# A fused attention and mixture-of-experts kernel: operands of x kept in SBUF over four experts, with tokens grouped by chunk position

## The chip, the cores and the metric

The kernel runs on one core of a Trainium2 chip. The metric is the device time of one execution in microseconds (us). Three runs of the kernel before took 1182.35, 1184.10 and 1184.86 us; the median, 1184.1 us, is the time that the change is measured against.

## The reference

The first half is a decayed linear attention, the second a weighted sum of four two-layer networks over its result. All data are 32-bit floats.

```python
# q, k, v: (4 sequences, 8 heads, 768 positions, 64); blocks of 64 positions, one after the other
intra = (qb @ kb.T * Dmask) @ vb            # within the block, Dmask[i, j] = lam ** (i - j) for i >= j
inter = (qb * lam_pow) @ kv_state           # from all blocks before; kv_state starts at zero
out_block = intra + inter
kv_state = lam_block * kv_state + (kb * rev_pow).T @ vb
# x = out, tokens by features: (3072, 512)
p = domain_probs / (domain_probs.sum(-1) + 1e-9)
out = sum(p[:, e:e+1] * (relu(x @ w1[e]) @ w2[e]) for e in range(4))   # w1: 512 x 1024, w2: 1024 x 512
```

## The kernel before, in words

**Tiling.** A chunk is 128 positions of one sequence, all eight heads: two blocks of the reference. There are 24 chunks, six for each sequence. Eight chunks (1024 tokens) make a group, and there are three groups. The chunks go sequence by sequence, so group 0 holds sequence 0 and the first two chunks of sequence 1. A chunk's attention has three parts, `turn` (q and k are transposed, by TensorE, or for eight late chunks by VectorE from rows that came through a DRAM tensor `across`; GpSimd scales k in `decayed`), `scores` (products of q and k, and of k and v for the state) and `values` (L627: L643 is the product of q with the carried state, L659 that of the scores with v). The result goes to the tile `xT` (L309), which holds one group.

**Two products, as Strassen schemes.** For a group g and an expert e, `first_product` (L897) makes relu(x @ w1) and `second_product` (L958) makes the product with w2 and adds it, times the gate, to the group's result (L986, L989). Each is a seven-product (Strassen-Winograd) scheme, M1 to M7, and each of first_product's seven is split in seven once more. So first_product needs for every M seven blocks of x (128 x 256 each) and seven of w1. These are differences and sums of blocks of the input. `prepare_x` (L314) and `inner_x` (L203) compute those of x on GpSimd, for group 0 `own_x` (L1231) does on VectorE, and all are stored to a DRAM tensor `x_ops` (L129). The weights' operands are prepared by GpSimd in the same way and stored to `w1_ops`. For every expert, group and M, `feed` (L824) fetches 896 KB of `x_ops` (L832) and then 896 KB of `w1_ops` (L834), each into a tile of a pool `stream` with two buffers for each kind.

The hidden result of first_product stays in SBUF in blocks A11, A12, A21, A22. `operands` (L706) makes S1 to S4 of them on VectorE as soon as a block is complete, in tiles of their own ("hS"), from a pool of 48 tiles. `second_product` takes these in the order SEQ2 (L939), M1, M2, M7, M6, M4, M5, M3. For the last group the second product is turned round and also split twice (`nested_product`, L1199).

**Order of the work.** The order on every engine is written out by the kernel; nothing is rescheduled. The units (group, expert) go one after the other. In each unit the second product of this unit is interleaved with the first product of the next: seven steps (one M of each), each of eight slots, in which four parts of the second product and seven of the first alternate (L1540). In each slot the loop also takes one piece of VectorE work from a list `background` (`rest`, L510), may run one step of the next group's attention (`attention`, L680, at places that PLACES, L678, lists by step and slot), and calls `pump` (L150). This starts the next piece of preparation ("chore") when a running estimate of GpSimd's busy time lets it, and issues stores that are due. At the first slot of a step, the operands of the next step's M are fetched (L1564). In unit 0 a list `own_sums` gives one subtraction of `own_x` a slot. Group 0's attention, at the start, is interleaved with the first parts of a plain seven-product scheme for expert 0 (`direct_product`), in a list by hand.

SP issues nearly all DMAs, in this order, and a DMA that has to wait for a buffer or for data holds those behind it. `give_across` (L1107) writes a part of the last group's result at the very end, transposed on VectorE and in eight DMAs for M3.

Of the kernel before, what the change touches and what calls it, by code (L numbers as in the profile page):

```python
# [17 lines left out]
NPOOL = 48  # L18
AHEAD = 2
# [3 lines left out]
def kernel(  # L23
# [30 lines left out]
    nc = tc.nc  # L54
# [20 lines left out]
    stage = ctx.enter_context(tc.tile_pool(name="stage", bufs=8))  # L75
    w2pool = ctx.enter_context(tc.tile_pool(name="w2", bufs=6))
    stream = ctx.enter_context(tc.tile_pool(name="stream", bufs=2))
    opool = ctx.enter_context(tc.tile_pool(name="o", bufs=CPG))
# [15 lines left out]

    def tt(eng, o, a, b, op):
        eng.tensor_tensor(out=o, in0=a, in1=b, op=op)  # L96
        if eng is nc.gpsimd:
            busy[0] = max(busy[0], now[0]) + math.prod(o.shape[1:]) / 480
# [10 lines left out]

    nat = {}  # L110

    def load(n, names="qkv"):

        b, c = divmod(n, NCH)
        for name in names:
            x = small(f"{name}n")
# [12 lines left out]
    x_ops = dram.tile([NG, 7, P, 7, 256], FP32, name="x_ops")  # L129
# [4 lines left out]
    X_AT = {n: i for i, n in enumerate(("M1", "M7", "M6", "M4", "M5", "M2", "M3"))}  # L134
# [67 lines left out]

    def inner_x(eng, g, m, blk):  # L203
        at = {"B11": (0, 0), "B12": (0, 1), "B21": (1, 0), "B22": (1, 1)}
        inner(eng, ("x", g, m), x_ops[g, MS.index(m)], blk, T_OPS, at)
# [103 lines left out]
    xT = consts.tile([P, 4, G], FP32, name="xT")  # L309

    b11, b21 = xT[:, 0:2, 0:W], xT[:, 2:4, 0:W]
    b12, b22 = xT[:, 0:2, W:G], xT[:, 2:4, W:G]

    def prepare_x(g):  # L314

        st = {}

        def total(name, a, b, op):
            t = stage.tile([P, 2, W], FP32, name="xo", tag="st")
            halves(t[:], a, b, op)  # L320
            st[name] = t[:]

        def ready(m, blk):
            inner_x(nc.gpsimd, g, m, blk)

        return [lambda: ready("M1", b11), lambda: ready("M2", b21)], [
            lambda: total("T1", b12, b11, ALU.subtract), lambda: ready("M5", st["T1"]),
            lambda: total("T2", b22, st["T1"], ALU.subtract), lambda: ready("M6", st["T2"]),
            lambda: total("T3", b22, b12, ALU.subtract), lambda: ready("M7", st["T3"]),
            lambda: ready("M3", b22),  # L330
            lambda: total("T4", b21, st["T2"], ALU.subtract), lambda: ready("M4", st["T4"]),
        ]


# [29 lines left out]
    ACROSS = {2: 2, 3: 2}  # L364
    across = dram.tile([B, 2, P, NHP, NCH * 4, 32], FP32, name="across")
    pieces = []

    def bring_across(b):
        c = ACROSS[b]
        for x, of in enumerate((q, k)):  # L370
            for y in range(4):
                for ac in range(NHP):
                    src = of[b, 4 * (y // 2) + ac, c * C:, (y % 2) * 32:(y % 2 + 1) * 32]
                    to = across[b, x, y * 32:(y + 1) * 32, ac, c * 4:]
                    pieces.append(lambda to=to, src=src: nc.sync.dma_start(
                        out=to, in_=src.rearrange("(t p) d -> p t d", p=32),
                    ))

    def trickle(m=1):
        for _ in range(m):  # L380
            if pieces:
                pieces.pop(0)()

    def comes_across(n):
        b, c = divmod(n, NCH)
        return b in ACROSS and c >= ACROSS[b]

    def load_across(n):
        b, c = divmod(n, NCH)
        for x, name in enumerate("qk"):  # L390
# [3 lines left out]
                in_=across[b, x, :, :, c * 4:c * 4 + 4].rearrange("p h t d -> p h (t d)"),  # L394
# [3 lines left out]
    def load_more(n):  # L398
        if not comes_across(n):
            load(n)  # L400
        else:
            trickle(len(pieces))
            load_across(n)
            load(n, "kv")
# [11 lines left out]
    zeros = xT[:, 3, G - P:]  # L416
# [15 lines left out]
    s_decay = consts.tile([P, 2, NHP, BL], FP32, name="s_decay")  # L432
# [11 lines left out]
    q_decay = consts.tile([P, NHP, BL], FP32, name="q_decay")  # L444
# [14 lines left out]
    def scale_q(qs, qT):  # L459
        by = q_decay[:].unsqueeze(2).to_broadcast([P, NHP, 2, BL])  # L460
# [6 lines left out]
    gate = consts.tile([P, NTOK // P, E], FP32, name="gate")  # L467


    gate_rows = dram.tile([CPG, E, P], FP32, name="gate_rows")  # L470
    gate_bc = xT[:, 0].rearrange("p (n t) -> p n t", t=C)
# [9 lines left out]

    def turn_gates():
        p, o = bank("s0", "gp"), small("gr")
        n = CPG * E
        nc.tensor.transpose(out=p[0:n, 0:P], in_=gate[:, LAST * CPG:].rearrange("p n e -> p (n e)"), identity=ident[:])
# [9 lines left out]
    background = []  # L495
    aside = []
# [17 lines left out]
    def soon(n, *work):  # L514

        background[0:0] = work
        if n < CPG:
            rest(len(work))

    def decayed(n):  # L520

        kn = nat[n, "k"]
        if comes_across(n):
            kd = kn
        else:
            kd = small("kd")[:].rearrange("p (h d) -> p h d", d=D)
# [6 lines left out]
    def begin_state(n):  # L533
        if n % NCH == 0 and n not in states:
            states[n] = small("kv")[:].rearrange("p (x h d) -> p x h d", x=2, d=D)
            nc.vector.memset(states[n][:, 0], 0.0)
        if n % NCH and n in states and n not in carried:
# [16 lines left out]
    def turn(n, tags):  # L554
# [5 lines left out]
        decayed(n)  # L560
        qn, kn = nat.pop((n, "q")), nat.pop((n, "k"))
        qp = bank(tags[0], "qp")
        kp = bank(tags[1], "kp")
        for x, y in ((qp, qn), (kp, kn)):
            for ac in range(NHP):
# [3 lines left out]
                )  # L569
        qT, kT, qs = small("qT"), small("kT"), small("qs")  # L570
# [6 lines left out]
    def scores(n, tags):  # L577
        all_added()
        while n not in turned:
            rest(force=True)  # L580
# [3 lines left out]
        first, last = n % NCH == 0, n % NCH == NCH - 1  # L584
# [33 lines left out]
        def end():  # L618
            s = states[n + 1] = small("kv")[:].rearrange("p (x h d) -> p x h d", x=2, d=D)
# [7 lines left out]
    def values(n, tags):  # L627
# [3 lines left out]
        st, work = masked.pop(n)  # L631
        while any(f in background for f in (*scaled, *work)):
            rest(force=True)
        state = states.pop(n)
        c = n % CPG
# [12 lines left out]
        for a in range(2):  # L648
            for r in range(2):
                inter(a, r, 1 - r, a == 0)  # L650
        for a in range(2):
            for r in range(2):
                inter(a, r, r, False)
        for r in range(2):
            for a in range(2):
                for x in range(2):
                    for y in range(2):
# [5 lines left out]
                        )  # L663
        for x in range(2):
            o = xT[:, :, c * C + x * BL:c * C + (x + 1) * BL]
            nc.scalar.copy(out=o, in_=op[x][:, 0:4 * BL].rearrange("p (a t) -> p a t", t=BL))
            o = o[:, 2 * (1 - x):2 * (1 - x) + 2]
            p = op[1 - x][:, 4 * BL:6 * BL].rearrange("p (a t) -> p a t", t=BL)
            adds.append((now[0], lambda o=o, p=p: tt(nc.vector, o, o, p, ALU.add)))

    FEW = tuple((i, 5) for i in range(7))
    MANY = (0, 5), (1, 2), (1, 5), (2, 5), (3, 2), (3, 5), (4, 5), (5, 2), (5, 5), (6, 5)
    WIDE = (0, 2), (0, 5), (1, 5), (2, 2), (2, 5), (3, 5), (4, 2), (4, 5), (5, 5)

    def places(**units):
        return [(int(at[1:]) * 7 + i, x) for at, of in units.items() for i, x in of]

    PLACES = {1: places(u0=FEW[2:], u1=MANY, u2=WIDE), 2: places(u3=FEW, u4=MANY, u5=MANY[:7])}  # L678

    def attention(g):  # L680

        steps = []
        early, late = prepare_x(g)
        for n in range(g * CPG, (g + 1) * CPG):
            steps.append(lambda n=n: turn(n, ("s0", "s1")))
            steps.append(lambda n=n: scores(n, ("s0", "s1")))

            def end(n=n):
                if n == g * CPG:
                    for m in MS:  # L690
                        until(("x", g - 1, m))
                values(n, ("s0", "s1"))
                if n + AHEAD < B * NCH:
                    load_more(n + AHEAD)
                if n % (CPG // 2) == CPG // 2 - 1:
# [906 lines left out]
```

## Time and profile before

| what | value |
|---|---|
| median of three runs | 1184.1 us |
| profiled execution, as a run | 1181.85 us |
| its span, first to last instruction | 1180.0 us |
| TensorE matmul busy | 98%, 8159 records |
| VectorE, ScalarE, GpSimd busy | 68%, 23%, 55% |
| DMA: moved, mean rate | 324.45 MB, 275 GB/s |
| share of the 16 DMA engines, SP's queue | 82.4% |
| mean granted TensorE clock | 0.997 |

A "record" is one instruction of the trace. A group of equal instructions has its place in the code, what it writes and reads, their shape and number; a wait names the engine and line that waited and what ended the wait, its total, how often, and the longest. In an answer in order of time, the first number is the start and the second the duration, both in us; "x8" means eight records merged, and square brackets hold the idle time of the engine ahead of them. PE is TensorE's matmul, PEld its weight load, DVE VectorE, ACT ScalarE, POOL GpSimd, SP the engine that issues DMAs, and SPq an issue. An issue's time on SP is short; the data land later (the page gives the median).

### The profile page before, as it was taken

How to read it: one execution, taken by the hardware profiler on the slowest of the kernel's cores; microseconds unless marked ns; L12 is line 12 of the kernel's file. 1: busy time of each engine (PE TensorE's matmuls, PEld its weight loads, DVE VectorE, ACT ScalarE, POOL GpSimd, SP SyncE). 2: the span in 40 equal slices, each digit the busy share in tenths (PEclk: the TensorE clock that was granted, in tenths of full speed). 3: DMA queues.
4: the chain of work that ended last, by engine and by line, in shares of the span. 5: the costliest groups of instructions: out<-in, count | busy, mean ns of one | idle time of the engine just before them, and what ended most of it. 6: DMA issues, size and time to landing. Idle time of an engine off the chain costs nothing.

```text
span 1180.0 us, 21215 instructions
## 1 busy us (share of the span) xinstructions
PE 1160.9 (98%) x8159; PEld 1009.9 (86%) x8159; DVE 798.7 (68%) x1411; ACT 275.2 (23%) x507; POOL 651.4 (55%) x624
## 2 busy tenths in 40 slices
PE   8999999999999899999999999999999999999998
PEld 7888888888878788888888888888888888888887
DVE  4796796678468647747856765764665676777785
ACT  3342122013111101311220120121243342341331
POOL 2848258347557920064445655416684683783884
PEclk9999999999999999999999999999999999999999
DMA  9798799999999997899998899898986657566543
GB/s 207 202 267 239 248 310 329 336 348 315 363 339 338 319 324 227 259 308 299 324 318 268 285 306 316 283 302 305 314 281 239 256 194 279 200 248 238 214 162 89
DMA packets 265621, 324.45 MB, mean 275 GB/s; under 512 B 121488, under 2 KB 206896, under 8 KB 265520
## 3 DMA queue, kind: packets, MB, share of 16 engines
q1 hardware_dynamic: 254912, 320.27, 82.4%
q10 hardware_dynamic: 10608, 2.82, 1.2%
q8 instruction: 65, 1.06, 0.4%
q14 instruction: 36, 0.29, 0.1%
HBM read 237.69 MB, written 89.54 MB: 277 GB/s over the span
## 4 chain that ended last, share of the span: by engine, by line
PE 86%; DMA 7%; DVE 4%; POOL 2%; issue 1%; SPq 0%; ACT 0%; ACTq 0%; DVEq 0%; POOLq 0%
PE pg L919 35%; PE q L973 28%; PE pq L1199 13%; PE pM L1334 2%; PE pc L1334 2%; DMA w2b<-in_moe_w_dram 2%; DMA ws_in<-w_ops 2%; POOL ops L96 1%; DVE m L96 1%; PE sp L591 1%; PE op L643 1%; DMA w_ops<-ops 1%; DMA w_sums<-w2o 1%; DMA w_ops<-w1o 1%; PE sp L598 1%; PE op L659 1%
## 5 line engine op out<-in xcount | busy, mean ns | idle before, releaser
L919 PE MATMUL pg<-xs_in,ws_in 128*128 128x256 f32 x1960 | 471.3, 380 | 6.7 <-DMA ws_in<-w_ops 6.4
L919 PEld LDWEIGHTS pg<-xs_in,ws_in 128*128 128x128 f32 x1960 | 371.9, 190 | 60.0 <-issue 5.0
L96 DVE TENSOR_TENSOR m<-pg,m 128x512 f32<-128x512 f32 x451 | 307.3, 687 | 98.2 <-PE pg L919 90.5
L973 PE MATMUL q<-w2t,hS 128*128 128x256 f32 x1024 | 243.5, 381 | 0.0
L973 PEld LDWEIGHTS q<-w2t,hS 128*128 128x128 f32 x1024 | 193.1, 190 | 26.5
L989 DVE SCALAR_TENSOR_TENSOR acc<-q,gate,acc 128x256 f32<-128x256 f32 x192 | 92.5, 482 | 162.4 <-PE q L973 162.0
L973 PE MATMUL q<-w2t,m 128*128 128x256 f32 x768 | 183.1, 381 | 0.0
L973 PEld LDWEIGHTS q<-w2t,m 128*128 128x128 f32 x768 | 145.0, 190 | 20.2
L931 ACT ACTIVATE m<-m 128x512 f32<-128x512 f32 x132 | 82.9, 631 | 281.0 <-DVE m L96 280.3
L96 POOL TENSOR_TENSOR m<-m,xT 128x512 f32<-128x512 f32 x64 | 80.6, 1275 | 73.6 <-ACT m L931 41.6
L96 DVE TENSOR_TENSOR sums<-pq,sums 128x256 f32<-128x256 f32 x153 | 64.2, 422 | 46.2 <-PE pq L1199 39.2
L96 POOL TENSOR_TENSOR ops<-w2b 128x256 f32<-128x256 f32 x24 | 18.8, 804 | 136.8 <-DMA w2b<-in_moe_w_dram 128.1
L927 ACT COPY m<-pg 128x512 f32<-128x512 f32 x88 | 51.6, 586 | 181.2 <-PE pg L919 170.4
L1199 PE MATMUL pq<-acc,w2t 128*128 128x256 f32 x352 | 86.6, 379 | 0.0
L1199 PEld LDWEIGHTS pq<-acc,w2t 128*128 128x128 f32 x352 | 66.8, 190 | 9.3 <-issue 0.3
L96 POOL TENSOR_TENSOR w2o<-w2b 128x512 f32<-128x512 f32 x32 | 41.0, 1303 | 44.5 <-DMA w2b<-in_moe_w_dram 25.9
L96 POOL TENSOR_TENSOR acc<-hT,hT 128x512 f32<-128x512 f32 x32 | 40.3, 1275 | 30.3 <-PE pq L1199 28.4
L862 ACT ACTIVATE m<-m 128x512 f32<-128x512 f32 x44 | 27.8, 631 | 106.5 <-DVE m L96 106.5
L96 DVE TENSOR_TENSOR hS<-m,m 128x512 f32<-128x512 f32 x56 | 44.7, 799 | 6.5 <-ACT m L931 6.5
L96 DVE TENSOR_TENSOR m<-m,m 128x512 f32<-128x512 f32 x56 | 48.2, 861 | 0.0
L96 POOL TENSOR_TENSOR acc<-hT,acc 128x512 f32<-128x512 f32 x32 | 40.7, 1273 | 7.4 <-PE pq L1199 5.4
L96 POOL TENSOR_TENSOR ops<-w1b 128x256 f32<-128x256 f32 x24 | 20.6, 878 | 43.6 <-PE pg L919 22.6
(166 smaller groups left out, 1375.7 us busy)
## 6 DMA issues: line engine op xcount, KB each, us to landing
xs_in<-x_ops SPq DMA_DIRECT2D x70, 896.0 KB, 6.4
ws_in<-w_ops SPq DMA_DIRECT2D x70, 896.0 KB, 8.4
w2t<-w_ops SPq DMA_DIRECT2D x66, 256.0 KB, 6.9
w2t<-w_sums SPq DMA_DIRECT2D x64, 256.0 KB, 4.2
w_ops<-ops SPq DMA_DIRECT2D x28, 512.0 KB, 7.3
w2t<-in_moe_w_dram SPq DMA_DIRECT2D x48, 256.0 KB, 4.4
w2b<-in_moe_w_dram SPq DMA_DIRECT2D x32, 256.0 KB, 6.0
w_sums<-w2o SPq DMA_DIRECT2D x16, 512.0 KB, 6.0
```

What stands on the lines that cost most here:

```text
L96: eng.tensor_tensor(out=o, in0=a, in1=b, op=op)
L591: nc.tensor.matmul(out=sp[r][half[x], ac * BL:(ac + 1) * BL], lhsT=hc(kT)[half[r], ac, blk[x]], rhs=hc(qT)[half[r], ac, blk[x]], start=(ac ...
L598: nc.tensor.matmul(out=sp[x][half[r], 256 + ac * D:256 + (ac + 1) * D], lhsT=kd[half[x], 2 * ac + r], rhs=vn[half[x], 4 * r + ac], start=F ...
L643: nc.tensor.matmul(out=op[r][half[y], cols(a, r) if x == r else apart(a)], lhsT=state[half[r], x, 2 * a + y], rhs=by_block(qs)[half[r], 2 ...
L862: nc.scalar.activation(out=o[:], in_=o[:], func=AF.Relu)
L919: nc.tensor.matmul(out=p[:, j * 256:(j + 1) * 256], lhsT=ws[i][:, j * P:(j + 1) * P], rhs=xs[i], start=(fresh and j == 0), stop=True, skip ...
L927: nc.scalar.copy(out=new[at][:], in_=p[:])
L931: nc.scalar.activation(out=new[at][:], in_=new[at][:], func=AF.Relu)
L973: nc.tensor.matmul(out=p[:, s * DH:(s + 1) * DH], lhsT=h[A_OF[m]][:, c * 256 + s * P:c * 256 + (s + 1) * P], rhs=fed2[g, e, m][uu][:, c], ...
L989: nc.vector.scalar_tensor_tensor(out=o, in0=x, scalar=w, in1=o, op0=ALU.mult, op1=ALU.add)
L1199: nc.tensor.matmul(out=p[:, 0:256], lhsT=fed3[e, m, x // 2][:, x % 2, c * P:(c + 1) * P], rhs=b[B_OF[i]][:, c * 256:(c + 1) * 256], start= ...
L1334: nc.tensor.matmul(out=p[:, s * 256:(s + 1) * 256], lhsT=a[c][:, f:f + P], rhs=b[:, c, j * 256:(j + 1) * 256], start=(s == 0 and c == 0 an ...
```

## The change

**Groups.** A group is now two chunk positions of all four sequences: chunks 0 and 1 of each in group 0, 2 and 3 in group 1, 4 and 5 in group 2. States of four sequences are carried side by side. Chunk position 0 has no state before it, so `values` leaves out that half of the product with the state. All chunks of group 2 come through `across`, in pieces for each sequence.

**Operands of x stay.** Seven tiles `slots`, one for each M, hold the seven blocks for first_product over all four experts. Group 0's attention writes into four of them directly, and `x_steps` makes the blocks by subtractions in place. For groups 1 and 2, `pair_sums` (GpSimd) makes the outer sums for every two chunks and stores them to `x_blocks` in DRAM; `x_fill` fetches one M's four blocks (two DMAs of 256 KB) into its slot after the last group's use of it, from step 18 and step 43 on, one M a step, and `x_inner` makes the inner differences on GpSimd. `feed` fetches weights alone.

**Room for it.** The common pool goes from 48 to 41 tiles and the stage pool from 8 to 7. The hidden operands are made in place: S3 over A21 when the block is complete, S2 over S3, S1 over A11 and S4 over A12 by `later_operands`, in the step after the last use of what they overwrite; SEQ2 is M1, M7, M4, M6, M2, M5, M3.

**Chunks at fixed distances.** An attention chunk's loads, turn, scores and values stand at fixed slots: 13 slots from chunk to chunk in group 1, 22 in group 2. Its VectorE work goes to a list `lately`, of which one piece is taken in each slot. k is scaled in place, after TensorE has transposed it.

**The end.** Output rows of a group are no longer contiguous over four chunks, so `give_across` writes each half by DMAs of its own, sixteen in place of eight.

```diff
-NPOOL = 48
-AHEAD = 2
+NPOOL = 41
...
+    xp = ctx.enter_context(tc.tile_pool(name="xp", bufs=1))
...
+    def token(g, half, x):
+        c, b = (half, x) if g == 0 else (2 * g + x % 2, 2 * (x // 2) + half)
+        return b * S + c * C
...
+    slots = {m: xp.tile([P, 7, 256], FP32, name="xs", tag="x" + m) for m in MS}
+    def x_steps(g, m, eng):
+        t = slots[m]
+        return [
+            lambda o=o, x=x, y=y: tt(eng, t[:, o], t[:, x], t[:, y], ALU.subtract)
+            for o, x, y in ((4, 3, 1), (1, 1, 0), (5, 3, 1), (6, 2, 5))
         ]
+    def x_inner(g, m):
+        for f in x_steps(g, m, nc.gpsimd):
+            f()
+        made.add(("x", g, m))
+
+    def x_fill(g, m):
+        for x in range(4):
+            until(("blocks", g, x))
+        slots[m] = xp.tile([P, 7, 256], FP32, name="xs", tag="x" + m)
+        for a in range(2):
+            nc.sync.dma_start(
+                out=whole(slots[m])[:, a].rearrange("p (x t) -> p x t", x=4),
+                in_=x_blocks[g - 1, :, :, BLOCK_AT[m], a * C:(a + 1) * C],
+            )
+        chores.insert(0, lambda: x_inner(g, m))
...
         for a in range(2):
             for r in range(2):
-                inter(a, r, 1 - r, a == 0)
+                if not first or r == 0:
+                    inter(a, r, 1 - r, a == 0)
...
+    def pair_sums(g, x, o):
+        s = stage.tile([P, 4, 256], FP32, name="to", tag="st")
+        (b12, b11), (b22, b21) = ((t[:, 0:256], t[:, 256:512]) for t in o)
+        for to, a, b in ((0, b12, b11), (1, b22, s[:, 0]), (2, b22, b12), (3, b21, s[:, 1])):
+            tt(nc.gpsimd, s[:, to], a, b, ALU.subtract)
...
+    FILL = {1: 18, 2: 43}
+    BEGIN = {1: (24, 13), 2: (8 * 19, 22)}
...
+            n, s = g * CPG + i, BEGIN[g][0] + BEGIN[g][1] * i
+            put(s - 10, lambda n=n: load_more(n))
+            put(s - 6, lambda n=n: load(n, "v"))
+            put(s, lambda n=n: turn(n, ("s0", "s1")))
+            put(s + (5 if comes_across(n) else 4), lambda n=n: scores(n, ("s0", "s1")))
+            put(s + (11 if comes_across(n) else 10), lambda n=n: values(n, ("s0", "s1")))
...
-        background.extend([
-            total("S3", "A11", "A21", ALU.subtract), total("S1", "A21", "A22", ALU.add, ("A21",)),
-            total("S2", "S1", "A11", ALU.subtract), total("S4", "A12", "S2", ALU.subtract),
-        ])
+        def step():
+            t = h["S3"] = h.pop("A21")
+            tt(nc.vector, t[:], h["A11"][:], t[:], ALU.subtract)
+        background.append(step)
+
+    def later_operands(g, e, m):
+        def step(h, a):
+            if m == "M4":
+                t = h["S2"] = h.pop("S3")
+                tt(nc.vector, t[:], a[:], t[:], ALU.subtract)
+            elif m == "M2":
+                t = h["S1"] = h.pop("A11")
+                tt(nc.vector, t[:], h["S2"][:], t[:], ALU.add)
+            else:
+                t = h["S4"] = h.pop("A12")
+                tt(nc.vector, t[:], t[:], h.pop("S2")[:], ALU.subtract)
+
+        if m in ("M4", "M2", "M5"):
+            for sj in (1, 0):
+                for uu in range(2):
+                    h = hid[g, e, uu, sj]
+                    background.append(lambda h=h, a=h["A22"] if m == "M4" else None: step(h, a))
...
     def feed(g, e, m):
-        until(("x", g, m))
         until(("w1", e, m))
-        xs = stream.tile([P, 7, 256], FP32, name="xs_in", tag="x")
-        nc.sync.dma_start(out=xs[:], in_=x_ops[g, MS.index(m)])
         ws = stream.tile([P, 7, 256], FP32, name="ws_in", tag="w")
         nc.sync.dma_start(out=ws[:], in_=w1_ops[e, MS.index(m)])
...
-    SEQ2 = ("M1", "M2", "M7", "M6", "M4", "M5", "M3")
+    SEQ2 = ("M1", "M7", "M4", "M6", "M2", "M5", "M3")
...
-        for a in range(4 * t):
+        for a in range(4):
...
+            if (g, e) < (LAST, 0):
+                later_operands(g, e, SEQ2[i])
...
+                take(lately)
                 if x % 2:
                     trickle()
+                for h in range(1, NG):
+                    if x == 3 and 0 <= at * 7 + i - FILL[h] < 7:
+                        x_fill(h, SEQ[at * 7 + i - FILL[h]])
```

## The prediction

> **What bounds the kernel now.** I read four views in this order: the busy times, TensorE's own waits, the order of time around its longest waits, and the waits of the engines that feed it.
>
> ```profile
> PE 1160.9 (98%) x8159; PEld 1009.9 (86%) x8159; DVE 798.7 (68%) x1411; ACT 275.2 (23%) x507; POOL 651.4 (55%) x624
> ```
>
> Busy time of TensorE (PE) leaves 1180.0 - 1160.9 = 19.1 us of idle time in the whole span. The next two rows of the order of time show that the busy part is dense: eight records start 1.73 us after the eight before them, 0.216 us each. (A matmul of the program stands as two records.)
>
> ```profile
> 725.94 1.89 PE L973 MATMUL q<-w2t,hS 128*128 128x256 f32 x8
> 727.67 1.89 PE L919 MATMUL pg<-xs_in,ws_in 128*128 128x256 f32 x8
> ```
>
> So the change can win idle time, or matmuls, and nothing else. TensorE's waits (total, times, longest) say where the idle time is:
>
> ```profile
> PE pg L919 <- DMA ws_in<-w_ops: 6.4, 3, 4.1
> PE pg L919 <- DVE m L96: 2.3, 3, 1.0
> PE op L659 <- issue: 2.2, 1, 2.2
> ```
>
> All rows of that view add up to 15.6 us; from the last matmul's end (1176.3) to the end of the span lie another 3.7. Around the two long DMA waits the order of time reads:
>
> ```profile
> 328.35 0.42 SPq L834 DMA_DIRECT2D ws_in<-w_ops  x1
> ...
> 337.21 1.96 PE L919 MATMUL pg<-xs_in,ws_in 128*128 128x256 f32 x8 [2.07 <-DMA ws_in<-w_ops]
> ```
> ```profile
> 403.80 0.32 SPq L832 DMA_DIRECT2D xs_in<-x_ops  x1
> 404.17 0.42 SPq L834 DMA_DIRECT2D ws_in<-w_ops  x1
> ...
> 410.68 3.46 PE L919 MATMUL pg<-xs_in,ws_in 128*128 128x256 f32 x8 [4.07 <-DMA ws_in<-w_ops]
> ```
>
> The weights come 8.9 and 6.5 us after their issue, always behind 896 KB of x operands. In the second case SP issued nothing from 399.2 to 403.8: the fetch of x waits for the store of the same operands (x_ops<-xo, issued up to 398.6), made by GpSimd (POOL) only then. And the eight records after that wait take 3.46 us, not 1.89: another 1.6 us lost.
>
> [...] after the wait of 4.07 us records are 0.43 us apart, after that of 2.07 they are not. [...] SP waited 5.1 us in three times for x_ops<-xo at L832. [...]
>
> **The change part by part.** Times are of the profiled execution: span 1180.0 us, 1181.85 us as a run; the median of the runs shown is 1184.1, so it lies 2.25 us above. I add one net difference to both.
>
> *x operands stay (removed).* 70 fetches of 896 KB (62.7 MB) go, and the stores of three groups' operands (21 x 896 KB); 14 fills of 512 KB and eight stores of 896 KB come. Most of this is worth nothing: in a plain step of 30 matmuls, 30 x 2 x 0.216 = 13.0 us, the weights are asked for a step ahead and land in 8.4 us (median), hidden. It is worth the two waits where issue was late: the first because half the bytes ahead of the weights are gone, the second because fetch no longer waits for store. I take all 6.4 us and the 1.6 us of slow clock: **-8.0**. Bounds: -5.7 (only the second goes, 4.07 + 1.6) and -8.0.
>
> *Fewer matmuls.* Chunk position 0 of each sequence has no state, so values() leaves out half of the L643 block. A block of 32 small records takes 0.51 us (329.47 to 329.98 in the order of time): 4 x 0.25 = **-1.0**. The group before had that saving in none.
>
> *VectorE early on.* M1's four subtractions (4.5 us between 40.6 and 53.4) move behind the first x sums, and of group 0's hidden blocks only S3 is computed at once. TensorE's waits for VectorE are 2.3 at L919 and 1.4 for the x sums, 3.7 in all. The moved work returns in the unit after, where VectorE is 78% busy (75.7 of 97 us from 88 to 185). I take **-1.5**; bounds -3.7 and +1.0.
>
> *Added wait 1: the fill on GpSimd.* x_inner waits for its fill, and on GpSimd behind it stand the other chores and the scaled k of a chunk. The built order shows the tight place: step 18, where chunk 16's k follows x_inner (4 x 0.72), w1o (2 x 1.25), ops (4 x 0.72), kv 0.6 and k 1.06: 10.0 us after landing. The fill is issued some five issues of 0.5 us into the step and lands in about 6.4 (the median of xs_in): k is ready near 19 us. Its scores stand 13 to 14 slots of 1.62 us into it: 21 to 22.7. A slack of about 3 us. But SP can be late: at 327.9 it was some 8 us into its step (the step that uses that load starts at 333.25, this one 13.0 and 1.1 of attention earlier); then TensorE waits 6 us, and 1.6 more by the clock. In the kernel before, the same chain just fits:
>
> ```profile
> 325.81 0.62 POOL L96 TENSOR_TENSOR kv<-kv,q_decay 128x256 f32<-128x256 f32 x1
> 326.39 1.06 POOL L96 TENSOR_TENSOR kn<-kn,s_decay 128x512 f32<-128x512 f32 x1
> ```
> ```profile
> 329.98 0.65 PE L598 MATMUL sp<-vn,kn 64*64 64x64 f32 x32
> ```
>
> I take **+1.5** (a quarter of 6); bounds 0 and +7.6. Queued behind the scores: all matmuls.
>
> *Added wait 2: hidden operands in place.* S2, S1 and S4 are now computed one step before use, over tiles that the step before has read, and not a unit ahead. It is the same number of VectorE instructions of 0.69 us. Four are due in each of three steps; by the list of background work the last S4 comes up at slots 6 to 8, one or two slots (1.6 to 3.2 us) before its matmul, and at the last unit of group 1, where the last group's sums share the list, it is forced out right at it. What speaks against waits is that VectorE follows closely:
>
> ```profile
> DVE acc L989 <- PE q L973: 162.0, 145, 8.4
> DVE m L96 <- PE pg L919: 90.5, 210, 3.6
> ```
>
> It waits for TensorE, so it has no backlog. I take **+2.0**, four forced ones at about 0.5; bounds 0 and +12 (24 steps x 0.5).
>
> *The end.* give_across issues its eight DMAs of M3 twice over, in halves. SP's row there:
>
> ```profile
> 1165.61 3.46 SPq L1119 DMA_DIRECT2D out_dram<-y  x6
> 1170.34 4.28 SPq L1100 DMA_DIRECT2D out_dram<-y  x5
> ```
>
> Six more on SP at 0.58 are 3.5 us; 1.3 us lie free before 1170.3 and more before 1175.4. I take **+0.5**; bounds 0 and +2.
>
> *At nothing.* ScalarE copies each result in four pieces for two (it is 23% busy; up to 0.3 us for each of eight chunks in group 0 if the copy ends last: 2.4). The across pieces become 128 for 64 on SP at 0.56 us, 36 us spread over 30 steps, in place of 70 fetches of 0.34. Fewer pool buffers: a load that waits for a buffer would hold the weights behind it on SP, but these have a margin of 13.0 - 8.4 = 4.6 us. Closer attention in group 1 (13 slots a chunk): scores come four slots, 6.5 us, after turn, where the tightest place before had three.
>
> Sum: -8.0 - 1.0 - 1.5 + 1.5 + 2.0 + 0.5 = **-6.5**: 1175.3 as the profiled run, 1177.6 against the median.
>
> **The rivals.** (a) *No new wait*: added waits 1 and 2 are zero: -10.0, 1174.1; as much of VectorE's 3.7 us as can go gives 1172. For it: VectorE is never behind. (b) *The wait moves to GpSimd*: the fill lands late, TensorE waits 6 + 1.6 us for k, S4 as forecast: -6.5 + 6.1 = -0.4, 1183.7. For it: GpSimd's in-order queue and 128.1 us of waits for w2b; against: TensorE's waits show none for GpSimd before. (c) *Slower: late operands.* In all 24 steps with in-place operands VectorE ends after TensorE needs them. The point: the forecast without wait 2 is -8.5, so an average of 0.45 us a step makes it slower than before by 2.4 us; at 0.8 us, 19.2, the time is 1184.1 - 8.5 + 19.2 = 1194.8. For it: these operands lose their lead of a step or more; against: VectorE's waits above. (d) *It doesn't take the transfers away*: excluded, the built program has no xs_in and 14 fills.
>
> **How the numbers follow.** The forecast 0.60, (a) 0.12, (b) 0.14, (c) 0.14. About 0.2% (2.4 us) is what this measurement tells from no change, so faster is below 1181.7 and slower above 1186.5. The forecast lies in faster; of (b) all counts as the same: faster 0.72, same 0.14, slower 0.14. The range runs from 1171 to 1187: (a) and (b) inside, (c) out, with some margin of the bounds on both sides.
>
> **What would show it.** Right: ws_in in no wait of TensorE over 1 us after 200 us and no half clock there; DMA busy share below 83% by about a fifth; small waits of L1012 (the second products) for VectorE, most at group 1's last unit; 32 fewer small matmuls (64 records). Wrong: a wait of scores for GpSimd over 3 us near the first chunk of group 2; waits of the second products for VectorE in every unit; TensorE idle above 19 us.

## The result, and the profile after

In twenty runs of each the changed kernel took 1180.99 us (median; 1176.3 to 1184.54) and the kernel before 1181.46 us (1179.04 to 1184.86). The ratio is 0.9993, with a 95% interval from 0.9983 to 1.0004: 2.0 us less to 0.5 us more, which is no change that can be told. The time lies in the forecast's range, but the forecast's gain of 6.5 us did not come. The median of before in twenty runs is also 2.6 us under that of the three runs on which the forecast was built. That shift has nothing to do with the change, and without it the measured time would lie further from the forecast's 1177.6 us: that it came within 3.4 us of it is luck.

The profiled execution of after has a span of 1178.8 us (1180.6 us as a run). Its page, busy times first, then the DMA queue that SP issues on and the one that brings instructions (packets, MB, share of 16 engines):

```profile
PE 1160.6 (98%) x8095; PEld 1008.8 (86%) x8095; DVE 798.2 (68%) x1407; ACT 271.0 (23%) x540; POOL 649.1 (55%) x640
...
q1 hardware_dynamic: 254976, 251.46, 68.6%
...
q8 instruction: 64, 1.05, 0.4%
```

The transfers are gone: 251 MB on SP's queue, for 320 before, and 68.6% of the DMA engines for 82.4%. The 64 PE records are gone too. Yet PE's idle time is 1178.8 - 1160.6 = 18.2 us, for 19.1 before. TensorE's waits in after (total, times, longest) say what took its place:

```profile
PE sp L621 <- issue: 2.8, 1, 2.8
PE op L693 <- issue: 2.0, 2, 1.9
PE pg L958 <- DVE m L102: 2.0, 3, 0.9
PE sp L628 <- POOL kn L102: 2.0, 2, 1.4
PE zp L443 <- DVE zeros L438: 1.1, 1, 1.1
PE gp L512 <- DVE kv L102: 1.0, 1, 1.0
```

No row for ws_in is left, where before had 6.4 us. New are 2.8 us of "issue" at L621, 2.0 us for GpSimd's k (kn), and 1.0 us for the transposition of gates (gp). Three places of after in order of time show them. The opening, PE alone:

```profile
34.97 0.65 PE L693 MATMUL op<-st,vn 64*64 64x64 f32 x32
35.44 0.63 PE L621 MATMUL sp<-qT,kT 64*64 64x64 f32 x29
38.83 0.37 PE L621 MATMUL sp<-qT,kT 64*64 64x64 f32 x2 [2.76 <-issue]
...
41.85 3.47 PE L1338 MATMUL pM<-xs,w1b 128*128 128x256 f32 x8
```

PE stops in the middle of a group of 32 equal matmuls, and the profile shows nothing that it waits for. After the stop eight records take 3.47 us, not 1.89: the clock is halved from 38.2 to 45.0 us. Before has a stretch of half clock in its opening too, of 3.4 us from 15.0 on, after its own stop:

```profile
14.92 0.73 PE L659 MATMUL op<-st,vn 64*64 64x64 f32 x18 [2.19 <-issue]
15.35 1.16 PE L643 MATMUL op<-qs,kv 64*64 64x64 f32 x32
```

After's stop at the same place, of 1.9 us, was followed by none.

The second place, near the first chunks of group 2, GpSimd and PE:

```profile
367.01 3.81 POOL L102 TENSOR_TENSOR xs<-xs 128x256 f32<-128x256 f32 x4 [13.02 <-PE pg L958]
...
377.99 1.07 POOL L102 TENSOR_TENSOR kv<-kv,decay 128x256 f32<-128x256 f32 x1
...
379.02 1.05 POOL L102 TENSOR_TENSOR kn<-kn,decay 128x512 f32<-128x512 f32 x1
...
380.13 0.69 PE L628 MATMUL sp<-vn,kn 64*64 64x64 f32 x32 [1.41 <-POOL kn L102]
```

GpSimd stands idle for 13.02 us before the x sums of a fill; then come the x sums, sums of weights, the state (kv) and only then k, on which PE waits. The third is the transposition of the gates (the four experts' factors p):

```profile
498.84 0.41 DVE L102 TENSOR_TENSOR kv<-kv,sp 128x256 f32<-128x256 f32 x1
...
499.40 0.27 PE L512 MATMUL gp<-ident,last_gate 128*32 128x128 f32 x1 [1.00 <-DVE kv L102]
```

Its result goes to a bank of PSUM, the pool that the kernel's matmuls write to, whose content VectorE has not yet added to the state.

To see where time goes, I split each trace into three parts: **opening**, to the start of record 110 (from 0) of the 128x256 matmuls; **middle**, on to the start of the last such record; **tail**, the rest. PE has 0.8 us less work before record 110 in after than in before.

| us | opening | middle | tail | span |
|---|---|---|---|---|
| before | 63.7 | 1109.5 | 6.8 | 1180.0 |
| after | 66.8 | 1105.8 | 6.2 | 1178.8 |

The change wins 3.7 us in the middle and 0.6 in the tail, and loses 3.1 in the opening.

### The profile page after: what moved, and what is told of

Read it like the earlier page. It is cut to its first block, busy times and chain, and to the rows that moved or that the text cites. A ratio compares the mean times of both kernels' runs of the same rounds, so it can differ in the third digit from the quotient of the medians.

```text
span 1178.8 us, 21191 instructions
## 1 busy us (share of the span) xinstructions
PE 1160.6 (98%) x8095; PEld 1008.8 (86%) x8095; DVE 798.2 (68%) x1407; ACT 271.0 (23%) x540; POOL 649.1 (55%) x640
## 3 DMA queue, kind: packets, MB, share of 16 engines
q1 hardware_dynamic: 254976, 251.46, 68.6%
## 4 chain that ended last, share of the span: by engine, by line
PE 92%; DVE 3%; POOL 2%; issue 1%; DMA 1%; ACT 0%; SPq 0%; ACTq 0%; POOLq 0%; DVEq 0%
PE pg L958 38%; PE q L1012 31%; PE pq L1238 13%; PE pM L1338 2%; PE pc L1338 2%; PE op L675 1%; PE sp L621 1%; PE sp L628 1%; PE op L693 1%; DVE m L102 1%; PE qp L593 1%; PE kp L593 1%; POOL xs L102 1%; DVE xs L102 1%; POOL acc L102 1%
## 5 line engine op out<-in xcount | busy, mean ns | idle before, releaser
L958 PE MATMUL pg<-xs,ws_in 128*128 128x256 f32 x1960 | 470.1, 380 | 1.2 <-DVE m L102 1.1
L1012 PE MATMUL q<-w2t,m 128*128 128x256 f32 x1792 | 426.1, 380 | 0.0
L958 PEld LDWEIGHTS pg<-xs,ws_in 128*128 128x128 f32 x1960 | 370.9, 190 | 54.2 <-DVE m L102 4.0
L1012 PEld LDWEIGHTS q<-w2t,m 128*128 128x128 f32 x1792 | 338.1, 190 | 46.8 <-DVE m L102 0.4
L102 DVE TENSOR_TENSOR m<-m,m 128x512 f32<-128x512 f32 x184 | 150.8, 820 | 9.7 <-ACT m L970 9.7
L102 POOL TENSOR_TENSOR m<-m,decay 128x512 f32<-128x512 f32 x64 | 81.9, 1296 | 59.6 <-ACT m L970 46.3
L102 POOL TENSOR_TENSOR xs<-xs 128x256 f32<-128x256 f32 x56 | 43.9, 785 | 78.1 <-DMA xs<-x_blocks 56.3
L1238 PEld LDWEIGHTS pq<-acc,w2t 128*128 128x128 f32 x352 | 66.8, 190 | 9.3 <-issue 0.3
L102 POOL TENSOR_TENSOR to<-xc 128x256 f32<-128x256 f32 x16 | 12.6, 786 | 109.7 <-DVE xc L102 46.9
L102 POOL TENSOR_TENSOR kn<-kn,decay 128x512 f32<-128x512 f32 x16 | 18.5, 1155 | 51.5 <-PE kp L593 29.9
L102 POOL TENSOR_TENSOR w2o<-w2b,w2o 128x512 f32<-128x512 f32 x24 | 34.0, 1444 | 13.5 <-DMA x_blocks<-to 9.8
```

The costliest lines, as they stand in the source:

```text
L958: nc.tensor.matmul(out=p[:, j * 256:(j + 1) * 256], lhsT=ws[i][:, j * P:(j + 1) * P], rhs=xs[i], start=(fresh and j == 0), stop=True, skip ...
L1012: nc.tensor.matmul(out=p[:, s * DH:(s + 1) * DH], lhsT=h[A_OF[m]][:, c * 256 + s * P:c * 256 + (s + 1) * P], rhs=fed2[g, e, m][uu][:, c], ...
L1238: nc.tensor.matmul(out=p[:, 0:256], lhsT=fed3[e, m, x // 2][:, x % 2, c * P:(c + 1) * P], rhs=b[B_OF[i]][:, c * 256:(c + 1) * 256], start= ...
```

## Experiments

My theory after the result (A): the two removed waits are worth what was forecast, and their gain is given back elsewhere. Its rival (B): without the waits the PE would only wait for VectorE or GpSimd in the same place. Times are compared with the kernel before, run beside each; differences from the changed kernel come from the two ratios to before. "Segments" are opening / middle / tail.

**The waits alone, in the kernel before**

```diff
+    kept, kept_x = [], {}
...
-        xs = stream.tile([P, 7, 256], FP32, name="xs_in", tag="x")
-        nc.sync.dma_start(out=xs[:], in_=x_ops[g, MS.index(m)])
+        k = (g, len(kept) % 2)
+        if k not in kept_x:
+            kept_x[k] = stream.tile([P, 7, 256], FP32, name="xs_in", tag="x")
+            nc.sync.dma_start(out=kept_x[k][:], in_=x_ops[g, MS.index(m)])
+        kept.append(m)
+        xs = kept_x[k]
```

> The kernel before with the x fetch of 896 KB left out except for the first two steps of each token group (6 fetches for 70; the products of the other steps then multiply stale x operands, so the values are wrong, the instructions of every engine the same). Theory A (the two PE waits for ws_in, 2.2 and 4.2 us of stall at 335 and 406 us, are worth what the trace shows, and the change gives their gain back elsewhere): no PE wait for ws_in above 0.5 us, no half clock at 411 us, 7.5 to 9 us less than before, 1172.5 to 1174 us. Theory B (the waits cover work on VectorE and GpSimd that is late as well, so without the fetch the PE waits for these): at most 2.5 us less, new waits of the PE for DVE or POOL between 330 and 420 us that sum to 4 us or more. Theory C (the profiled execution of before waited longer than a usual one): 3 to 5 us less.

Measured: 1172.53 us for 1181.13, ratio 0.9935 (0.9922 to 0.9947). Segments 62.6 / 1100.4 / 7.1. PE's longest waits are now

```profile
PE pg L924 <- DVE m L96: 2.3, 3, 1.0
PE op L659 <- issue: 1.9, 1, 1.9
```

No ws_in, no half clock at 411 us, and the wait for DVE is as long as in before. A holds; B and C fall: the waits are worth 8.6 us by the two medians and 7.7 by the ratio, and nothing stands behind them. In the trace 1.1 of 9.9 us lie in the opening, which had no half clock here.

**The traffic put back, in the changed kernel**

```diff
+    fed_x, spare = [], [dram.tile([P, 7, 256], FP32, name=f"spare{i}")[:] for i in range(4)]
...
+        x2 = spare[len(fed_x) % 4]
+        fed_x.append(m)
+        nc.sync.dma_start(out=x2, in_=w1_ops[e, MS.index(m)])
         ws = stream.tile([P, 7, 256], FP32, name="ws_in", tag="w")
```

> The changed kernel, and ahead of each ws_in fetch on the same queue a copy of 896 KB from the same tensor into a spare DRAM tensor: the traffic of the removed x fetch, without any reader. Theory A (the traffic of the x fetch was what made ws_in late): DMA busy share from 69% to 83% or more, PE waits for ws_in of 4 to 8 us in all, 5 to 10 us slower than the changed kernel without it. Theory B (ws_in was late for another reason, its place in the queue or its buffer): DMA share up as well, PE waits for ws_in under 1 us, time within 2 us of the changed kernel.

Measured: 1218.38 us, ratio 1.0321 (1.0307 to 1.0335), some 39 us more than the changed kernel where A had 5 to 10. The DMA share rose to 79%, not to the 83% of before. The waits:

```profile
PE pg L962 <- DMA ws_in<-w_ops: 13.0, 6, 5.5
PE sp L628 <- POOL kn L102: 10.8, 3, 5.3
```

The direction is A's, the size is not: a copy from DRAM to DRAM is not the fetch of before, and PE now also waits 10.8 us for k. That traffic makes ws_in late is shown; how much of the 8.6 us is traffic and how much the order of store and fetch (in before SP issued nothing for 4.6 us) is not.

**k scaled four slots earlier**

```diff
     def turn_across(n):
-        decayed(n)
...
+            if comes_across(n):
+                put(s - 4, lambda n=n: decayed(n))
             put(s, lambda n=n: turn(n, ("s0", "s1")))
```

> The changed kernel with the scaling of k by the decay of the eight chunks that come transposed (GpSimd, 1.06 us each) issued four slots (6.5 us) earlier than the turn. Theory A (in group 2 the added x sums stand in GpSimd's queue ahead of this k, and the PE waits for it): the waits of L628 for kn (2.0 us in two places, with 0.7 us beside each) go, 2.5 to 3.5 us less than the changed kernel, some 3 us less than before. Theory B (something else in the same places is as late: the bank, the x transposes on VectorE, the state): the wait changes its name and at most 1 us is gained.

Measured: 1177.75 us, ratio 0.9972 (0.9961 to 0.9983), 2.5 us less than the changed kernel. Segments 66.9 / 1104.5 / 6.2. The kn rows are gone, but only 1.2 us of the gain lies in the middle of this trace (which is of the slowest of the seven runs), since a wait for VectorE takes the first place:

```profile
372.33 2.94 POOL L102 TENSOR_TENSOR w1o<-w1b 128x512 f32<-128x512 f32 x2
372.48 1.66 DVE L102 TENSOR_TENSOR m<-m,m 128x512 f32<-128x512 f32 x1
...
377.61 1.99 PE L959 MATMUL pg<-xs,ws_in 128*128 128x256 f32 x8 [1.49 <-DVE m L102]
```

The sum of two SBUF tiles takes 1.66 us beside GpSimd's; in after such a sum with no GpSimd instruction at the same time took 0.68 us. So both theories hold in part: k was late, and VectorE is late in the same place as well.

**No x sums at all**

```diff
-        slots[m] = xp.tile([P, 7, 256], FP32, name="xs", tag="x" + m)
...
-        chores.insert(0, lambda: x_inner(g, m))
+        made.add(("x", g, m))
```

> The changed kernel without the four subtractions on GpSimd per x fill (56 in all, 44 us of GpSimd): products of groups 1 and 2 multiply stale inner x operands in four of seven places, so the values are wrong. Theory A (the added x sums are what delays the k of chunks 16 and 18): the kn waits go, 2.5 to 3.5 us less than the changed kernel. Theory B (the w1 sums and the state's copy that stand beside them on GpSimd delay k, x sums or not): kn waits of over 1 us stay, less than 1 us gained.

Measured: 1177.84 us, ratio 0.9968 (0.9958 to 0.9979), 3.0 us less than the changed kernel. Segments 65.0 / 1102.0 / 6.2: 3.7 us less in the middle, no kn row. So the added x sums cost some 3 to 3.7 us, of which the forecast had 1.5.

**The saved matmuls made again**

```diff
+            nc.vector.memset(states[n][:, 0], 0.0)
...
-                if not first or r == 0:
-                    inter(a, r, 1 - r, a == 0)
+                inter(a, r, 1 - r, a == 0)
...
-                if not first or r == 1:
-                    inter(a, r, r, first and a == 0)
+                inter(a, r, r, False)
```

> The changed kernel with one part undone: the products of the first four chunks with their zero state are made again (32 matmuls, 64 PE records, the states set to zero ahead). Theory A (the PE of the changed kernel stops at a boundary of 256 PE instructions, 1474 from the start, for a block of instructions that came late; what the saved matmuls moved against these boundaries is what put a dense stretch of small matmuls behind a late block): with the stream as long as before the stop at 36 us and its half clock go, 3 to 4 us less, with 1.0 us of matmuls more, net 2 to 3 us less than the changed kernel, 1178 us. Theory B (the block is late for the traffic of the loads, whatever the count): stop of 2 to 3.5 us between 30 and 40 us stays, 1.0 us more than the changed kernel, 1182 us.

Measured: 1180.45 us for 1182.3, ratio 0.9983 (0.9975 to 0.9992). Segments 65.9 / 1106.7 / 6.2. Neither theory: the stop at 36 us is gone, but another has come, at 44 us, just ahead of the 1986th PE instruction:

```profile
43.60 0.60 PE L594 MATMUL kp<-ident,kn 128*128 128x128 f32 x4
46.22 1.02 PE L1337 MATMUL pM<-xs,w1b 128*128 128x256 f32 x4 [2.02 <-issue]
```

With 1.0 us of matmuls more the kernel is not slower. The saving is real as work, but smaller than what the stops move.

**Half a block of instructions more**

```diff
     warm(10)
+    few = bank("g1", "zp")
+    for _ in range(32):
+        nc.tensor.matmul(out=few[:, 0:16], lhsT=zeros, rhs=zeros[:, 0:16], start=True, stop=True)
```

> The changed kernel with 32 more warm-up matmuls of 16 columns right at the start, where the PE waits for q (128 PE instructions, half a block; no work is left out). Theory A (place of the boundaries in the stream): the stops move to other places of the stream, that at 36 us goes or is under 1 us, 2 to 4 us less than the changed kernel, 1177 to 1179 us. Theory B (traffic): the PE stops 128 instructions earlier in the same work, between 30 and 40 us, for 2 to 3.5 us, time within 1 us of the changed kernel.

Measured: 1188.54 us, ratio 1.0051 (1.0032 to 1.0069). The edit was not free, as I had thought it would be: the 64 added records took 11.4 us and held up everything, so the time says nothing. For its question one row remains: PE stops again just ahead of its 1474th instruction, now in another group of matmuls:

```profile
44.77 0.68 PE L678 MATMUL op<-qs,kv 64*64 64x64 f32 x29
46.91 0.27 PE L678 MATMUL op<-qs,kv 64*64 64x64 f32 x2 [1.46 <-issue]
```

So here the stop, of 2.76 us in after and 1.46 in this run, belongs to the count of instructions, not to what they compute. B said so, but for B's reason, the traffic, this run shows nothing.

**k early, and the x sums one by one**

```diff
-        chores.insert(0, lambda: x_inner(g, m))
+        chores[0:0] = [*x_steps(g, m, nc.gpsimd)[0:3], lambda: (x_steps(g, m, nc.gpsimd)[3](), made.add(("x", g, m)))]
```

(and k scaled four slots earlier, as above)

> The kernel with the early k scaling, and the four x sums of a fill as four pieces of GpSimd work, planned one by one, where they were issued in a block of 3.8 us. Theory A (the block of sums delays what stands behind it on GpSimd, and VectorE's sums from SBUF beside it): the PE waits for DVE m at 376 and 388 us (2.4 us in the two places of the early-k kernel) shrink to under 1 us in all, 1 to 1.5 us less than the early-k kernel. Theory B (the total of GpSimd's work matters, not its grouping): within 0.5 us of the early-k kernel.

Measured: 1187.29 us, ratio 1.0042 (1.0028 to 1.0056). A miss for both. The two waits that the edit aimed at stayed (1.0 and 1.5 us), the later work of GpSimd moved, and at the start of the last group a chain over four engines is late:

```profile
869.89 3.79 POOL L102 TENSOR_TENSOR m<-m,decay 128x512 f32<-128x512 f32 x3
871.18 0.59 ACT L823 COPY hp<-m 128x512 f32<-128x512 f32 x1 [12.94 <-POOL m L102]
...
871.80 0.69 DVE L102 TENSOR_TENSOR hT<-hp,m 128x512 f32<-128x512 f32 x1 [7.73 <-ACT hp L823]
...
874.38 2.07 PE L959 MATMUL pg<-xs,ws_in 128*128 128x256 f32 x4 [5.85 <-DVE m L102]
```

A half clock of 3.4 us follows. In after this place costs 0.9 us: 0.3 at 872 for VectorE, and 0.7 at 874 with no releaser in the profile. In before it costs nothing.

**The x sums one step later**

```diff
-        chores.insert(0, lambda: x_inner(g, m))
...
+                    if x == 3 and 0 <= at * 7 + i - FILL[h] - 1 < 7:
+                        chores.insert(0, lambda h=h, m=SEQ[at * 7 + i - FILL[h] - 1]: x_inner(h, m))
```

> The changed kernel with one edit: the four x sums of a fill go into GpSimd's work one step (13 us) after the fill's transfers are issued, not at once; they are needed two steps after that. Theory A (the loss in group 2 is a queue effect: GpSimd stands idle before the x sums, up to 13 us for the slot's last reader and up to 10.9 us for the transfer, with k, the state's copy and the weight sums behind it): GpSimd's idle time before xs (69 us in all) falls under 15 us, the kn waits (2.0 us) go, 2 to 3.7 us less than the changed kernel, as much as without the sums at all. Theory B (the sums' 44 us of work is what costs): kn or DVE m waits of 2 us or more stay between 370 and 460 us, less than 1 us gained.

Measured: 1178.89 us for 1182.21, ratio 0.9973 (0.9963 to 0.9983), 2.4 us less than the changed kernel. Segments 66.0 / 1104.5 / 6.2. There is no kn row in PE's waits, with the same sums made. GpSimd's idle time before them:

```profile
POOL xs L102 <- DMA xs<-x_blocks: 30.2, 6, 11.1
```

In after it was 56.3 us for the DMA and 13.0 for PE. It is not under 15 us, as A had it, but at the tight place k now stands ahead of the x sums:

```profile
364.18 1.06 POOL L102 TENSOR_TENSOR kn<-kn,decay 128x512 f32<-128x512 f32 x1
...
368.51 3.98 POOL L102 TENSOR_TENSOR xs<-xs 128x256 f32<-128x256 f32 x4
```

So the wait for k, 2.0 us in after, was one of order in a queue, not of work. How much of the whole loss is order stays open: by time this edit wins 2.4 of the 3.0 us that leaving the sums out wins, by the middles of the two traces 1.3 of 3.7. Stalls of 0.9 us at 387 and of 0.9 at 870 remain here.

**Three edits together**

```diff
+            if comes_across(n):
+                put(s - 4, lambda n=n: decayed(n))
...
+    steps.append((256, turn_gates))
+    steps.sort(key=lambda s: s[0])
...
-            if e == 0:
-                chores.append(turn_gates)
```

(and the x sums one step later, as above)

> The changed kernel with the x sums one step later, the k scaling of the transposed chunks four slots earlier, and the transposition of the last group's gates at a fixed slot between two chunks (it waited 1.16 us for a bank that a chunk's state still held). If the three losses are separate: 1.0 to 1.2 us less than with the x sums later alone (no gp wait at 498 us) and up to 0.7 us from k, 4 to 5 us less than the changed kernel, about 1176 us. Rival: the planner's later GpSimd work moves against the start of the last group (as when the sums were planned apart: 5.8 us of wait at 868 us) and takes it back.

Measured: 1177.11 us for 1182.21, ratio 0.9966 (0.9954 to 0.9978), 3.2 us less than the changed kernel where 4 to 5 were expected. Segments 68.8 / 1102.6 / 6.2. No gp row: the gates' loss is gone. The middle is 3.1 us shorter than in after. The opening of this trace is the longest but that with the extra warm-up.

**Less to load in the opening**

```diff
+        if (e, name) == (0, "A22"):
+            w1_now[e][name] = w1_now[e]["A21"]
+            return
```

> The changed kernel with one load left out in the opening: the 512 KB of the weight quarter A22 of the first expert, issued at 32 us; A21 is read in its place, so the values are wrong and the instructions of every engine but two DMA issues the same. Theory A [...]: the fetch that started at 36.6 us starts by 34 us, the stop at 36 us is under 1 us, the 110th large matmul some 3 us earlier than 66.8 us, 2 to 4 us less than the changed kernel. Theory B (the stop does not hang on this traffic): stop of 2 us or more at a boundary between 30 and 40 us, the 110th large matmul at 65 to 67 us, within 1 us of the changed kernel.

Measured: 1180.2 us for 1181.78, ratio 0.9988 (0.9979 to 0.9997). Segments 66.8 / 1106.2 / 6.3. The block for the 1474th instruction again started at 36.7 us, and PE stopped three times after the first stop (1.6, 1.2 and 2.4 us from matmul to matmul). So A, that the loads issued just ahead of this block make it late, falls for this load. B's single stop of 2 us or more between 30 and 40 us did not come either; its time and its opening did.

**The edits with another load order**

```diff
-        (vs[0], loads("A22")), (vs[1], loads(7)),
+        (vs[0], loads(7)), (vs[1], loads("A22")),
```

> The kernel with the three edits in group 2, and in the opening the load of the weight quarter A22 issued after the loads of the eighth chunk, not ahead of them (no work left out). Theory A (the stops of the PE in the opening hang on what is loaded just ahead of a block of instructions): the stop at the 1474th instruction changes by over 1 us, and the time with it; as the traffic ahead of the block is as large (640 KB for 512 KB), the direction is open. Theory B: opening as before the edit, 110th large matmul at 65 to 69 us, time within 1 us of the three edits alone (0.9966 of before).

Measured: 1176.32 us for 1181.78, ratio 0.9954 (0.9938 to 0.9971). Segments 68.0 / 1102.5 / 6.2. The stop at the 1474th instruction fell from 3.0 us, with the three edits alone, to 1.1, as A has it, but one of 1.9 came at the 1730th, and the opening is within B's bounds. The interval overlaps that of the three edits alone, so the order of loads is not shown to matter to the time. It is the fastest version here that leaves no work out, 5.4 us below before by the ratio.

**The kernel before once more**

No edit.

> The kernel before, unchanged, for a third profile of its opening. Theory A (the changed opening itself meets its blocks of PE instructions later): one stop of some 2.3 us at the 449th PE instruction, none over 1.5 us at a later boundary before 60 us, the 110th large matmul at 62.5 to 64 us as in the two profiles with this opening. Theory B (the stops fall by chance in either opening): a later stop of 2 us or more, the 110th large matmul at 65 us or later, as in nine of the ten profiles with the changed opening.

Measured: one run, 1181.35 us. Segments 63.5 / 1109.0 / 7.0, and one "issue" wait of more than a microsecond:

```profile
PE op L659 <- issue: 2.2, 1, 2.2
```

The opening of before took 63.7, 62.6 (with x kept) and 63.5 us in three profiles, mean 63.3; the changed opening, in the ten profiles without the extra warm-up, 63.6 to 68.8, mean 66.5. Three of these ten had a small edit in the opening (saved matmuls made again, a load left out, a load moved), and one had added traffic. PE's waits with no releaser there add up to 2.7, 2.7 and 3.0 us in the three and to 4.6 to 8.1 in the ten, mean 5.8. A holds: some 3 us are lost there, by such stops. But the shortest of the ten, 63.6 us with the x sums apart, has the opening of after unchanged, so the loss varies from one execution to the next.

## Why the prediction was right and wrong

Right were the bound (98% busy before and after), the sum of the waits removed and the sign of most terms. The time lay in the range, but that says little: the range also held no change at all. Wrong was the net gain. By its terms:

| term | forecast | measured |
|---|---|---|
| x operands stay | -8.0 | -7.7 to -8.6 (the waits alone) |
| fewer matmuls | -1.0 | 64 records of work; made again, not slower |
| VectorE early on | -1.5 | about -0.8: two stalls of 1.1 and 1.2 us at 133 and 159 us became 0.5 and 1.0 at 94 and 137 |
| wait 1, the fill on GpSimd | +1.5 | +3.0 (no x sums, by time) to +3.7 (its middle) |
| wait 2, operands in place | +2.0 | 0: no idle time ahead of L1012 |
| end | +0.5 | -0.6 |
| gate transposition | not in the sum | +1.2 |
| opening | at nothing | +3.2 (means; +3.1 in the first trace of each), the saved matmuls included |

**The step that failed first is "at nothing".** There the forecast costed group 0's opening by its copies and left it at that; that PE can run out of instructions there was not seen, though before showed it: the row "op L659 <- issue: 2.2" is among the lines that the forecast shows, and was left unexplained. Counting all of PE's records (matmuls, weight loads and semaphore waits), the first stop lies just ahead of PE's 450th instruction in each of these traces but that of the extra warm-up; the later ones of 1474 and 1986, and those with the load left out (1218, 1474, 1730), differ from it by whole blocks of 256. The instruction queue agrees: in after it brought 64 packets of 16.4 KB for PE's 16522 records, 258 each; and in before and after alike the first fetch had ended before PE's 450th record ran, the second before the 706th, and so on by 256 to the end, at all 127 such places, by 1.27 us or more (median some 16). The margin was smallest in the openings, where small matmuls use up a block in some 4.5 us: in after the fifth fetch, the one ahead of the 1474th instruction, started at 36.6 us, when PE had stopped at 36.1; in before the fifth started at 33.1, and PE passed that place at 36.6 without a stop. The openings of the fourteen traces have 31 stops of 0.9 us or more with no releaser, and in each PE goes on 1.1 to 1.7 us after a fetch on that queue has ended. Why it starts later in most profiles of the changed opening stays open. With the saved matmuls made again it started at 34.1, but another block was late; leaving out one load and reordering two left it at 36.7 and 36.1.

**Wait 1 was right in its mechanism, and mis-sized.** The forecast saw k behind the x sums at step 18, priced one late chunk at a quarter of 6 us, and named a wait over 3 us as its refutation. The longest was 1.4. But it came for two chunks, not one, and other stalls cost about as much again: PE's wait for VectorE's m at 376 and 389 us (0.7 each) and the last group's start (0.9). Without the x sums the first and the last of these are gone; that at 389 is not (0.9 at 385), and a new one of 0.7 stands ahead of L1011 at 856. A way from GpSimd's sums to VectorE's lateness is in the trace. In after, VectorE's sums of two SBUF tiles (m<-m,m, 128x512) took 681 ns where no GpSimd instruction ran at the same time (95 of them, longest 694), but up to 1728 ns beside one (89, median 924); those with a PSUM operand (m<-pg,m) had a median of 691 ns in either case. Why the sums of two SBUF tiles are the ones that take longer is not shown. That these durations make up the stalls is read from the trace, and no run separates the two.

**Wait 2 was too dear.** The profile of after has, with the idle time before it in the last column:

```profile
L1012 PE MATMUL q<-w2t,m 128*128 128x256 f32 x1792 | 426.1, 380 | 0.0
```

That VectorE waits for PE, which the forecast showed, was the better evidence: it had the time even for operands that come just before use.

**The rivals.** The outcome has the size of (b), 0.4 us gained, but not its one place: no wait of 6 us, no half clock in group 2. Rival (c) is refuted by L1012, (a) by kn. "The same" had 0.14; two losses that could add, GpSimd and something in the opening, would have deserved more.

**The clock.** The forecast set the wait of 4.07 us, after which records were 0.43 us apart, beside that of 2.07, after which they were not. It left out the half clock of before at 15.0 us, which came after a stop of 2.2 us. Of the five stops over 1.5 us in the traces of before and after, those of 2.19, 2.76 and 4.07 us were followed by a half clock, those of 1.88 and 2.07 were not. What halves the clock is not shown.

**The signs named beforehand.** Right: no wait for ws_in over 1 us, the DMA share 17% lower (68.6 for 82.4), 64 records fewer. Not seen: small waits of L1012 for VectorE. Of the signs of a wrong forecast none came: the scores' wait was 1.4 us, not over 3, and PE was idle for 18.2 us, not over 19. They looked at group 2 and at the whole idle time, while the half clock in the opening (6.8 us) is busy time to PE; none looked at the opening.

The sum of the terms leaves some 1 us of the middle that is not assigned, and the time itself is known to about 1.2 us.

## What to carry to other kernels

A wait for a transfer on the busiest engine is worth its length when nothing else is late in the same place (7.7 to 8.6 us here, for 6.4 of waits and 1.6 of half clock); take it away alone, before the rest of a change, to know. Work put into an engine's queue ahead of its data can cost what stands behind it (GpSimd stood idle for 13.0 us before a fill's x sums, and issuing the sums one step later took 2.4 us off the time): issue it when its data are there. When a wait has no releaser in the profile, count the engine's own instructions up to it in two traces before costing that stretch at nothing.

## What the runs showed of the hardware

- PE ran out of instructions in the opening: it stopped for 1.0 to 3.3 us, with no releaser in the profile, at whole blocks of 256 of its records from its first stop, and went on 1.1 to 1.7 us after a fetch of instructions had ended, in or just after stretches of 64x64 matmuls, where 32 records take about 0.5 us.
- After a stop of 2.76 us the clock was halved for 6.8 us; after one of 1.9 us at 12.9 us in the same trace it was not. In before it was halved for 3.41 us after a stop of 2.2 us. From PE's first attention matmul to its last matmul the half clocks of the two traces lasted 3.41 and 3.41 us in before and 6.83 in after.
- 64 records of 16 columns took 11.4 us, 0.18 us each in the mean, with weights of 128x128: one every 0.11 us at full clock, every 0.21 at half. The records of 128 columns just before them came at the same two distances. So here fewer columns made a matmul no cheaper.
